# A fused attention and token-mixing block on one core: the last two blocks normalised by transposes into one tile, a ninth buffer for exponentials, and one planner policy for every stretch

## Chip, core and metric

The kernel runs on one core of one Trainium2 chip. The metric is the device time of one execution in microseconds (us), as the median of several runs. One execution was also taken by the hardware profiler. Its span is the time from the program's first to its last profiled instruction.

## What is computed

One token sequence of S = 2048 rows and D = 512 columns is normalised twice and goes through multi-head attention (32 heads of 16 columns) and through a token-mixing MLP of width F = 1376. The results are added to the input:

```python
def _A_ref(x, wqkv, wo):
    B, S, D = x.shape
    H = 32; Dh = D // H
    qkv = (lambda x, *d: x.transpose(*d))((x @ wqkv).reshape(B, S, 3, H, Dh), 2, 0, 3, 1, 4)
    q, k, v = qkv[0], qkv[1], qkv[2]
    scores = jnp.einsum("bhqd,bhkd->bhqk", q, k) * Dh ** -0.5
    p = _softmax(scores, axis=-1)
    o = jnp.einsum("bhqk,bhkd->bhqd", p, v)
    return (lambda x, *d: x.transpose(*d))(o, 0, 2, 1, 3).reshape(B, S, D) @ wo

def _B_ref(x, w1, b1, w2, b2):
    h = _layernorm(x, axis=-1)
    u = _gelu(jnp.einsum("bsd,sf->bdf", h, w1) + b1)
    y = jnp.einsum("bdf,fs->bds", u, w2) + b2
    return (lambda x, *d: x.transpose(*d))(y, 0, 2, 1)

xn = _layernorm(A_x, axis=-1)
return A_x + _A_ref(xn, A_wqkv, A_wo) + _B_ref(xn, B_w1, B_b1, B_w2, B_b2)
```

Inputs, weights and the output are bfloat16.

## The kernel before

**Blocks and groups.** Queries are cut into 4 quarters of 512 rows (qb), heads into 8 sets of four (G). That makes 32 blocks (NBLK), numbered b = 8 qb + G. T = G // 2 is a tile of 128 columns of the heads' output, and e_ = G % 2 says which half of each 32 rows of that tile the block fills. A block has 16 groups (NKT), one for each 128 keys, 512 groups in all. A group's scores are four matmuls (score_mm, L678), one for each head, and each fills one PSUM bank of 512 columns.

**Two paths for the exponentials.** A group goes one of two ways. On ScalarE it takes two ACTIVATE instructions (exp_tile, L701), each over two banks, into one of NPB = 8 buffers of pT; two more buffers lie in xn_sb once that tile is free (NPX = 2), which the profile shows as `xn_sb<-ps` on L701. The other path approximates the exponential with integer arithmetic on the bits of bfloat16 numbers: VectorE copies each of the four banks with a scale and a bias into a "plane" (dve_first, L761, or two banks at once in dve_first2, L769), and two further planes are made by adding a constant, by VectorE (add_plane, L774) or GpSimd (add_plane_pool, L781). Planes lie in tiles that have become free (x_sb, xn_sb, plx, h_sb, w1blk, wqkv_sb, xnT). TensorE then multiplies each buffer, or each of the three planes, by V (pv_mm, L714), four 32-column matmuls at a time, and adds up in PSUM bank 6 (PV_BANK). V17 has a column of ones for each head, so row 16 of each 32 rows of the sum is the softmax denominator. V17b is the same, scaled for the third plane.

**The order.** The order of all instructions is worked out on the host when the program is built: a dispatcher steps a clock for each engine, with an estimated occupancy and latency for each operation, and appends an instruction to its engine's stream when its inputs should be there. On the chip each engine runs its stream in order and waits on semaphores. pe_step decides what TensorE does next: scores for ScalarE if one of ScalarE's two PSUM slots should be free, scores for the other path if a bank of 4, 5 and 7 is, or else a "unit" of four 32-column matmuls (a PV product, a step of a projection, of the MLP or of the output projection; pe_fill). A tuple of 16 numbers (TOL, JOIN, DEFER and so on) sets tolerances and preferences. POLICY holds such a tuple for every 10 us of planned time (SEG), 65 in all. Which groups go which way falls out of this: ScalarE takes the next group whenever it can, d_pick1 chooses for the other path.

**Between the blocks.** chain_epi normalises a block: VectorE copies PV_BANK into OT32 (cp, L1286); SP gathers the four denominator rows through DRAM into den_s, 16 numbers on each of 128 partitions (gather, gather2; LAT_I is the planner's latency for the latter); VectorE takes the reciprocal (L1301); SP writes it back and broadcasts it into denb (out1, and bcast with four DMAs); GpSimd multiplies OT32 by denb (L1323), for e_ = 0 into oT, for e_ = 1 into otmp, from where four DMAs (join, o_join) put it beside the other half in oT. Queries are brought to rows of QT by eight DMAs (q_rows).

**The end.** For the last four row tiles (12 to 15, here c = 0 to 3), chain_yo adds the MLP's result, the first PT[c] of four pieces of the output projection and the input into part. The remaining pieces (op_mm, T = PT[c] to 2) are added in bank TBANK[c]. For c in HL the value of part is split into a high and a low bfloat16 half on GpSimd (part_split) and added by two matmuls with the identity (part_mm), so that ScalarE can copy the bank out; for the others VectorE adds part on the way out (L2028). The last piece, T = 3, comes from blocks 30 and 31 in two products with zero-padded halves of the weights (op_half with wo_pad): e_ = 0 reads block 30's result in oT, e_ = 1 reads block 31's in otmp. Block 31 has no DMA chain: tail_epilogue transposes PV_BANK in 32 x 32 pieces (L1994), so that the denominators stand beside their numbers, takes reciprocals (L1999), multiplies into gT (L2003) and transposes back into otmp (L2008). The rows of the output go out by SP, the last by ScalarE's queue.

The gelu of the MLP runs once, in the middle, as two ACTIVATEs (L1062) between two loads of ScalarE's function tables.

## Time and profile before

| | |
|---|---|
| median of 3 runs | 657.51 us (657.49 to 657.55) |
| the profiled execution's own time | 657.41 us |
| its span | 655.6 us, TensorE's granted clock 0.999 |
| ScalarE (ACT) busy | 643.6 us, 98% |
| TensorE (PE) busy | 643.7 us, 98% |
| VectorE (DVE) busy | 616.6 us, 94% |
| GpSimd (POOL) busy | 424.2 us, 65% |

Busy times are unions: instructions of one engine that overlap are counted once. Matmuls are pipelined, so TensorE's share is no measure of its load. PEld are its weight loads. A row of the costliest groups gives the line, the engine, the operation, what it writes and reads with shapes, the count, the busy time and the mean of one instruction in ns, and, behind the second bar, the idle time just ahead of them with what ended it. A row of the timeline gives the start, the duration in us, the line and how many equal instructions were merged.

### The profile page before, as it was taken

To read this page: it belongs to the slowest core of one execution; us is meant where nothing else is said; L and a number is where in the kernel's file an instruction comes from. 1 tells how busy PE (TensorE), PEld (TensorE's weight loads), DVE (VectorE), ACT (ScalarE), POOL (GpSimd) and SP (SyncE) were. 2 spreads that over 40 slices of the span, in tenths; PEclk is the share of its full clock that TensorE was granted. 3 is DMA by queue.
4 is the path that set the end of the run, shared out by engine and by line. 5 is a ranking of instruction groups with operands and counts; after the bars stand their busy time and mean duration, and the time that the engine had idled before them with its cause. 6 is when DMAs were issued, how large, how long until landed. Compare 5 with 4: busy or idle time off the path is not lost.

```text
span 655.6 us, 20689 instructions
## 1 busy us (share of the span) xinstructions
PE 643.7 (98%) x8873; PEld 189.8 (29%) x8873; DVE 616.6 (94%) x1071; ACT 643.6 (98%) x702; POOL 424.2 (65%) x292
## 2 busy tenths in 40 slices
PE   8999999999999999999999999999999999999997
PEld 4533333322222222222222222222222222222222
DVE  7989999989999999999999999999999999999997
ACT  7999999999999999999999999999999999999996
POOL 5631567575675657554856877977787566676772
PEclk9999999999999999999999999999999999999999
DMA  7015110122222212220122222112011131312101
GB/s 225 4 52 110 28 41 4 31 51 54 56 44 58 51 28 55 51 40 19 29 57 54 56 57 57 43 45 70 22 50 26 32 78 34 90 43 59 36 24 51
DMA packets 77002, 32.99 MB, mean 50 GB/s; under 512 B 61618, under 2 KB 72818, under 8 KB 76910
## 3 DMA queue, kind: packets, MB, share of 16 engines
q1 hardware_dynamic: 76478, 31.27, 19.0%
q8 instruction: 70, 1.15, 0.7%
q10 hardware_dynamic: 432, 0.39, 0.2%
q14 instruction: 22, 0.18, 0.1%
HBM read 26.08 MB, written 2.61 MB: 44 GB/s over the span
## 4 chain that ended last, share of the span: by engine, by line
ACT 76%; PE 19%; DVE 2%; DMA 1%; POOL 0%; issue 0%; DVEq 0%; POOLq 0%
ACT pT L701 74%; PE ps L678 7%; PE ps L714 7%; PE ps L611 5%; ACT gT L1062 1%; ACT xn_sb L701 1%; DMA den_s<-den_scr 0%; DVE stats L528 0%; DMA x_sb<-in_A_x_dram 0%; POOL mv L549 0%; DVE xn_sb L566 0%; DMA den_scr<-OT 0%; DVE x_sb L761 0%; ACT L701 0%; ACT L1062 0%
## 5 line engine op out<-in xcount | busy, mean ns | idle before, releaser
L701 ACT ACTIVATE pT<-ps 128x1024 bf16<-128x1024 f32 x682 | 626.9, 1136 | 1.1 <-PE ps L678 0.9
L678 PE MATMUL ps<-QT,KT 32*128 32x512 bf16 x2048 | 277.4, 384 | 6.7 <-ACT pT L701 5.0
L678 PEld LDWEIGHTS ps<-QT,KT 32*128 32x128 bf16 x2048 | 71.4, 90 | 280.3 <-ACT pT L701 267.5
L714 PE MATMUL ps<-pT,V 128*32 128x512 bf16 x1364 | 132.4, 388 | 0.1
L761 DVE TENSOR_SCALAR x_sb<-ps 128x512 int16<-128x512 f32 x190 | 125.0, 684 | 7.8 <-PE ps L678 6.2
L761 DVE TENSOR_SCALAR xn_sb<-ps 128x512 int16<-128x512 f32 x140 | 92.6, 685 | 6.6 <-PE ps L678 5.3
L761 DVE TENSOR_SCALAR plx<-ps 128x512 int16<-128x512 f32 x104 | 68.5, 684 | 4.5 <-PE ps L678 3.8
L611 PE MATMUL ps<-h_sb,w1blk 128*32 128x512 bf16 x688 | 57.7, 383 | 0.0
L611 PE MATMUL ps<-gT,w2blk 128*32 128x512 bf16 (+1 forms) x704 | 56.2, 383 | 0.1
L714 PEld LDWEIGHTS ps<-pT,V 128*32 128x32 bf16 x1364 | 33.8, 94 | 62.6 <-issue 59.4
L761 DVE TENSOR_SCALAR xnT<-ps 128x512 int16<-128x512 f32 x72 | 47.4, 685 | 2.2 <-PE ps L678 1.5
L761 DVE TENSOR_SCALAR wqkv_sb<-ps 128x512 int16<-128x512 f32 x68 | 44.7, 684 | 2.1 <-PE ps L678 1.6
L611 PE MATMUL ps<-xnT,wqkv_sb 128*32 128x512 bf16 (+2 forms) x568 | 40.4, 355 | 0.1
L761 DVE TENSOR_SCALAR w1blk<-ps 128x512 int16<-128x512 f32 x56 | 36.1, 684 | 2.4 <-PE ps L678 2.1
L714 PE MATMUL ps<-x_sb,V 128*32 128x512 bf16 x380 | 36.1, 383 | 0.0
L781 POOL TENSOR_TENSOR x_sb<-x_sb,shift_w 128x1024 int32<-128x1024 int32 x14 | 26.5, 1891 | 14.3 <-DVE x_sb L761 6.3
L781 POOL TENSOR_TENSOR x_sb<-xn_sb,shift_w 128x1024 int32<-128x1024 int32 x9 | 17.0, 1892 | 25.7 <-PE ps L678 18.3
L781 POOL TENSOR_TENSOR xn_sb<-x_sb,shift_w 128x1024 int32<-128x1024 int32 x13 | 24.5, 1893 | 7.6 <-DVE plx L774 2.8
L714 PE MATMUL ps<-xn_sb,V 128*32 128x512 bf16 x292 | 28.7, 383 | 0.0
L1323 POOL TENSOR_TENSOR oT<-OT,denb 128x512 bf16<-128x512 f32 x16 | 20.4, 1275 | 12.5 <-DVE w1blk L774 7.0
L781 POOL TENSOR_TENSOR x_sb<-plx,shift_w 128x1024 int32<-128x1024 int32 x11 | 20.8, 1891 | 10.7 <-DVE plx L761 3.6
L761 DVE TENSOR_SCALAR h_sb<-ps 128x512 int16<-128x512 f32 x40 | 26.2, 685 | 1.4 <-PE ps L678 1.2
(197 smaller groups left out, 883.2 us busy)
## 6 DMA issues: line engine op xcount, KB each, us to landing
denb<-rec_scr SPq DMA_DIRECT2D x124, 64.0 KB, 2.0
w1blk<-in_B_w_dram SPq DMA_DIRECT2D x10, 512.0 KB, 5.4
w2blk<-in_B_w_dram SPq DMA_DIRECT2D x16, 320.0 KB, 3.3
xres<-in_A_x_dram SPq DMA_DIRECT2D x16, 128.0 KB, 2.2
QT<-qst SPq DMA_DIRECT2D x120, 16.0 KB, 1.8
out_dram<-osb SPq DMA_DIRECT2D x14, 128.0 KB, 1.7
wqkv_sb<-in_A_wqkv_dram SPq DMA_DIRECT2D x3, 384.0 KB, 7.8
x_sb<-in_A_x_dram SPq DMA_DIRECT2D x2, 512.0 KB, 6.8
```

Source lines behind the costliest of these rows:

```text
L611: return e.matmul(dst[a:b, :], lhsT=lhsT[:, a:b], rhs=rhs, start=start, stop=stop, **pos)
L678: return sc.add("pe", lambda e: e.matmul(bank(bk), lhsT=KT[32 * r:32 * r + 32, T, 128 * kt:128 * (kt + 1)], rhs=QT[32 * r:32 * r + 32, slo ...
L701: return sc.add("act", lambda e: e.activation(pT_buf(buf), ps[:, slot * 1024:(slot + 1) * 1024], ACTF.Exp, scale=EXP_SCALE), reads=[("bank ...
L714: return sc.add("pe", lambda e: e.matmul(bank(PV_BANK)[32 * r:32 * r + 32, :], lhsT=vt_[:, off:off + 32], rhs=rhs, start=start, stop=stop, ...
L761: return sc.add("dve", lambda e: e.tensor_scalar(plane_i[pb][:, 512 * r:512 * (r + 1)], bank(bk), BIAS, 0.0, ALU.add, ALU.max), reads=[("b ...
L781: return sc.add("pool", lambda e: e.tensor_tensor(plane_w[pb], plane_w[pb0], shift_w[:, j:j + 1].broadcast_to([128, 1024]), ALU.add), read ...
L1062: op = sc.add("act", lambda e, m=m, f0=f0, f1=f1: e.activation(gT[0:m, f0:f1, :], gT[0:m, f0:f1, :], ACTF.Gelu_apprx_tanh), reads=[("gT", ...
L1323: op = sc.add("pool", lambda e: e.tensor_tensor(dst, OT32[:, eb, :], denb[:, :], ALU.mult), reads=[("OT32", eb)] + [("denb", r) for r in r ...
```

## The change

- NPB is 9 instead of 8: one more buffer of pT.
- POLICY holds one tuple, used for all of planned time, in place of 65.
- The planner's estimates: a DMA occupies its queue for 632 ns in q_rows and o_join and for 560 ns in den_g (name of gather), where it was 450 for all; LAT_I is 3800 ns instead of 4300.
- Block 30 is normalised by chain_turn instead of chain_epi: VectorE transposes PV_BANK into denb, takes the reciprocal and multiplies into columns 0 to 15 of each 32 of otmp's second half. Block 31's result goes into columns 16 to 31 of the same tile, and two transposes bring both blocks together into oT. The last piece of the output projection is then one product with wo_c (op_last) for each of the four row tiles; wo_pad, its memset and its eight loads go.
- HL is (0, 2) and PT is (1, 2, 1, 2): row tiles 0 and 2 go out by ScalarE, 1 and 3 by VectorE, and a split waits for its own part alone (part_of).
- In tail_epilogue the remaining output matmuls are all put ahead of the last products.

```diff
@@ -57,7 +57,7 @@
 BITS_MAX = float(0x7F80)
 
 DEBUG_SCHED = False
-NPB = 8
+NPB = 9
 NPX = 2
 NQS = 4
 NW1 = 2
@@ -94,73 +94,7 @@
 
 
 SEG = 10000.0
-POLICY = [
...
-]
+POLICY = [(120.0, 200.0, 400.0, -1, 0, 1300.0, 0.0, 0.05, 2, 3, 2, 7500.0, 0, 0.0, 1000.0, 2)]
 
 
 SWITCH = 95.0
@@ -376,7 +310,6 @@
         wqkv_sb = wqkv_flat[:, :].rearrange("p (j c n) -> p j c n", j=3, c=NCT)
         qmask = sb("qmask", [128, 2], F32)
         wo_c = sb("wo_c", [128, 4, D], BF16)
-        wo_pad = sb("wo_pad", [128, 2, D], BF16)
         KT = sb("KT", [128, 4, S], BF16)
         QT = sb("QT", [128, NQS, 512], BF16)
         V17 = sb("V17", [128, NKT * H * 17 + 16], BF16)
@@ -433,7 +366,8 @@
             else:
                 def fn(eng, dst=dst, src=src):
                     return eng.dma_start(dst, src)
-            op = sc.add(q, fn, reads=reads, writes=writes, name=name, dma=True, out_dma=out_dma, occ=450.0, lat=lat)
+            op = sc.add(q, fn, reads=reads, writes=writes, name=name, dma=True, out_dma=out_dma,
+                        occ={"q_rows": 632.0, "o_join": 632.0, "den_g": 560.0}.get(name, 450.0), lat=lat)
 
             dma_free[0] = max(dma_free[0], op.start + 1300.0) + move
             op.end = max(op.end, dma_free[0] + 700.0)
@@ -442,7 +376,7 @@
 
         NPRE = 4
         TABLE = 1490.0
-        LAT_I, LAT_B = 4300.0, 3100.0
+        LAT_I, LAT_B = 3800.0, 3100.0
 
 
         sc.add("pool", lambda e: e.memset(ident[:], 0.0), writes=[("ident",)], occ=200, lat=430)
@@ -506,16 +440,9 @@
         MLAST = F - 128 * NFTF
 
         def late_consts():
-            sc.add("pool", lambda e: e.memset(wo_pad[:], 0.0),
-                   writes=[("wo_pad", e_, r) for e_ in range(2) for r in range(4)], occ=900)
             sc.add("dve", lambda e: e.memset(gT[96:97, NFT - 1, :], 1.0), writes=[("gT1",)], occ=500)
             dma("sp", wo_c[:, :, :], A_wo.rearrange("(T q) n -> q T n", q=128), reads=[], writes=[("wo_c",)],
                 name="ld_wo")
-            for e_ in range(2):
-                for r in range(4):
-                    row = 3 * 128 + 32 * r + 16 * e_
-                    dma("sp", wo_pad[32 * r:32 * r + 16, e_, :], A_wo[row:row + 16, :], reads=[],
-                        writes=[("wo_pad", e_, r)], name="ld_wop")
             sc.add("pool", lambda e: e.memset(b1r[:], 0.0), writes=[("b1r",), ("b1r2",)], occ=120, lat=230)
             dma("sp", b1r[0:NFT - 1, :], B_b1[0:128 * (NFT - 1)].rearrange("(ft p) -> ft p", p=128),
                 reads=[], writes=[("b1r",)], name="ld_b1a")
@@ -907,6 +834,7 @@
         ge_done = [1e18]
         yo_done = {qb: 0 for qb in range(NQB)}
         part_done = [0]
+        part_of = set()
         oT_done = {qb: set() for qb in range(NQB)}
         mul_done = [0]
         bc_done = [0]
@@ -1080,19 +1008,17 @@
             return mm(bank(bk), oT[:, par, T, 128 * sti:128 * (sti + 1)], wo_c[:, T, :], first, last,
                       [("oT", par, T), ("wo_c",)] + [("oTj", par, T, r) for r in range(4)], [("bank", bk)])
 
-        def op_half(par, e_, sti, bk, first, last):
-            src = oT[:, par, 3, 128 * sti:128 * (sti + 1)] if e_ == 0 else otmp[:, par_o(NBLK - 1), 128 * sti:128 * (sti + 1)]
-            key = ("oT", par, 3) if e_ == 0 else ("otmp", par_o(NBLK - 1), sti)
-            return mm(bank(bk), src, wo_pad[:, e_, :], first, last, [key] + [("wo_pad", e_, r) for r in range(4)],
+        def op_last(sti, bk):
+            return mm(bank(bk), oT[:, 1, 3, 128 * sti:128 * (sti + 1)], wo_c[:, 3, :], False, True, [("oTL", sti), ("wo_c",)],
                       [("bank", bk)])
 
         def par_o(b):
             return (b // 2) % 2
 
 
-        HL = (0, 1)
-
-        PT = (1, 1, 2, 2)
+        HL = (0, 2)
+
+        PT = (1, 2, 1, 2)
         TBANK = (4, 5, EX_BANK, 0)
         hl_done = [0]
         hilo = xnT_flat[:, 2048 * (NQB - 1):].rearrange("p (t n) -> p t n", n=512)
@@ -1174,6 +1100,7 @@
                                 writes=[("part", sti)] + [("h", t) for t in range(4 * sti // 2, 4 * sti // 2 + 2)],
                                 **T_DVE(512))
                     part_done[0] += 1
+                    part_of.add(sti)
                     return op
 
                 def gate():
@@ -1342,6 +1269,32 @@
             if e_ == 1:
                 steps.append(Step("sp", join))
             return Chain("epi%d" % b, steps, -1.0, 0.0)
+
+
+
+        def chain_turn(b):
+            dn = denb[:, :].rearrange("p (c m) -> p c m", m=32)
+            wt = otmp[:, 1, :].rearrange("p (c m) -> p c m", m=32)
+            dk = [("denb", r) for r in range(4)]
+
+            def cp():
+                op = sc.add("dve", lambda e: e.transpose(denb[:, :], bank(PV_BANK)), reads=[("bank", PV_BANK)], writes=dk,
+                            **T_DVE(512))
+                pv_block[0] = b + 1
+                pv_open[0] = True
+                return op
+
+            def rec():
+                return sc.add("dve", lambda e: e.reciprocal(den_s[:, 0, :], dn[:, :, 16]), reads=dk, writes=[("den_s", 0)],
+                              occ=100, lat=230)
+
+            def mul():
+                mul_done[0] += 1
+                return sc.add("dve", lambda e: e.tensor_tensor(
+                    wt[:, :, 0:16], dn[:, :, 0:16], den_s[:, 0, :].rearrange("p (c o) -> p c o", o=1).broadcast_to([128, 16, 16]),
+                    ALU.mult), reads=dk + [("den_s", 0)], writes=[("otmp", 1, c) for c in range(4)], two=True, **T_DVE(256))
+            return Chain("epi%d" % b, [Step("dve", cp, 610, gate=lambda: mul_done[0] >= b), Step("dve", rec, 100),
+                                       Step("dve", mul, 340, two=True)], -1.0, 0.0)
 
 
         ex_queue.append(chain_k1(-2.0))
@@ -1375,7 +1328,7 @@
             yo_pos[12 + i] = (28.05 + 0.75 * i, 0.75)
         for idx, st in enumerate(yt_order):
             ex_queue.append(chain_yo(st, yo_pos[st][0] + yo_pos[st][1], yo_pos[st][0], idx))
-        bg.append(Chain("hilo", [Step("pool", lambda c=c, j=j: part_split(c, j), gate=lambda c=c: part_done[0] >= (2 if c < 2 else 4)
+        bg.append(Chain("hilo", [Step("pool", lambda c=c, j=j: part_split(c, j), gate=lambda c=c: c in part_of
                                       and (NQB - 1, 3) in qt_done) for c in HL for j in range(2)], NBLK - 1.0, 0.0))
         bg.append(Chain("gelu", [Step("act", gelus, gate=lambda: ut_done[0] == NFT)], 0.0, 0.0))
         bg.append(chain_ln2r(1.0))
@@ -1427,8 +1380,6 @@
                     z.append((bk, lambda c=c, bk=bk, j=j: part_mm(c, j, bk),
                               lambda c=c, j=j: hl_done[0] > HL.index(c)
                               and sc.ready(reads=[("hilo", HL.index(c), j)]) <= now[0]))
-            z.append((bk, lambda c=c, bk=bk: op_half(1, 0, c, bk, False, False),
-                      lambda: len(oT_done[3]) == NG - 1 and sc.ready(reads=[("oT", 1, 3)]) <= now[0]))
             tail["steps"].append(z)
 
         def d_over():
@@ -1659,7 +1610,7 @@
             if last:
                 pv_open[0] = False
                 if b < NBLK - 1:
-                    bg.append(chain_epi(b))
+                    bg.append(chain_turn(b) if b == NBLK - 2 else chain_epi(b))
                     bg[-1].t = sc.streams["pe"][-1].end
                     bg[-1].due = -1.0
 
@@ -1977,47 +1928,40 @@
 
 
         def tail_epilogue():
-            b = NBLK - 1
-            po = par_o(b)
 
             NB = 256 // 32
             dt = pT[:, 0, :].bitcast(F32)
             dn = dt.rearrange("p (c m) -> p c m", m=32)
-            wt = gT[:, 0, :].rearrange("p (c m) -> p c m", m=32)
+            wt = otmp[:, 1, :].rearrange("p (c m) -> p c m", m=32)
 
             def half(hf):
                 cols, blks = slice(256 * hf, 256 * hf + 256), slice(NB * hf, NB * hf + NB)
-                return (cols, blks, den_s[:, 0, blks], ("denT", hf), ("denS", hf), ("gTt", hf))
+                return (cols, blks, den_s[:, 1, blks], ("denT", hf), ("denS", hf), ("wt", hf))
 
             for hf in range(2):
                 cols, blks, rc, dk, sk, wk = half(hf)
                 sc.add("dve", lambda e, cols=cols: e.transpose(dt[:, cols], bank(PV_BANK)[:, cols]),
-                       reads=[("bank", PV_BANK)], writes=[dk] + ([("pT", 0)] if hf == 0 else []),
-                       **T_DVE(256))
+                       reads=[("bank", PV_BANK)], writes=[dk] + ([("pT", 0)] if hf == 0 else []), **T_DVE(256))
             for hf in range(2):
                 cols, blks, rc, dk, sk, wk = half(hf)
                 sc.add("dve", lambda e, rc=rc, blks=blks: e.reciprocal(rc, dn[:, blks, 16]), reads=[dk],
-                       writes=[sk] + ([("den_s", 0)] if hf == 0 else []), occ=100, lat=230)
+                       writes=[sk] + ([("den_s", 1)] if hf == 0 else []), occ=100, lat=230)
             for hf in range(2):
                 cols, blks, rc, dk, sk, wk = half(hf)
                 sc.add("dve", lambda e, rc=rc, blks=blks: e.tensor_tensor(
-                    wt[:, blks, 0:16], dn[:, blks, 0:16], rc.rearrange("p (c o) -> p c o", o=1).broadcast_to([128, NB, 16]),
-                    ALU.mult), reads=[dk, sk], writes=[wk] + ([("gT", 0)] if hf == 0 else []), **T_DVE(128))
+                    wt[:, blks, 16:32], dn[:, blks, 0:16], rc.rearrange("p (c o) -> p c o", o=1).broadcast_to([128, NB, 16]),
+                    ALU.mult), reads=[dk, sk], writes=[wk], **T_DVE(128))
             for hf in range(2):
                 cols, blks, rc, dk, sk, wk = half(hf)
-                sc.add("dve", lambda e, cols=cols: e.transpose(otmp[:, po, cols], gT[:, 0, cols]), reads=[wk],
-                       writes=[("otmp", po, c) for c in (2 * hf, 2 * hf + 1)], **T_DVE(256))
-
+                sc.add("dve", lambda e, cols=cols: e.transpose(oT[:, 1, 3, cols], otmp[:, 1, cols]),
+                       reads=[wk] + [("otmp", 1, c) for c in (2 * hf, 2 * hf + 1)],
+                       writes=[("oTL", c) for c in (2 * hf, 2 * hf + 1)]
+                       + ([("oT", 1, 3)] + [("oTj", 1, 3, r) for r in range(4)] if hf == 0 else []), **T_DVE(256))
             for z in tail["steps"]:
-                while len(z) > 1:
+                while z:
                     z.pop(0)[1]()
-            for hf in range(2):
-                tr = sc.streams["dve"][hf - 2].end
-                for z in list(tail["steps"]):
-                    while z and (z[0][0] in TBANK[2 * hf:2 * hf + 2] or sc.free["pe"] + 226.0 <= tr):
-                        z.pop(0)[1]()
-                for c in (2 * hf, 2 * hf + 1):
-                    op_half(1, 1, c, TBANK[c], False, True)
+            for c in range(4):
+                op_last(c, TBANK[c])
             for c in range(4):
                 st = 12 + c
                 bk = TBANK[c]
```

65 rows, old and new, of the table POLICY are left out of this document.

## The prediction, made before the changed kernel was run

> **What bounds the kernel now.** I read the page first: busy time, the chain that ended last and the costliest group.
>
> ```profile
> span 655.6 us, 20689 instructions
> ...
> PE 643.7 (98%) x8873; PEld 189.8 (29%) x8873; DVE 616.6 (94%) x1071; ACT 643.6 (98%) x702; POOL 424.2 (65%) x292
> ...
> ACT 76%; PE 19%; DVE 2%; DMA 1%; POOL 0%; issue 0%; DVEq 0%; POOLq 0%
> ...
> L701 ACT ACTIVATE pT<-ps 128x1024 bf16<-128x1024 f32 x682 | 626.9, 1136 | 1.1 <-PE ps L678 0.9
> ```
>
> Three engines look full, but the chain is ScalarE's exponentials (L701): these 682 and four into a spare tile, 686 in all. They overlap, so the mean of one (1136 ns) is not its price. ScalarE's own timeline and waits say how tightly they stand:
>
> ```profile
> 9.99 50.98 ACT L701 ACTIVATE pT<-ps 128x1024 bf16<-128x1024 f32 x55 [0.21 <-PE ps L678]
> ...
> 629.71 18.57 ACT L701 ACTIVATE pT<-ps 128x1024 bf16<-128x1024 f32 x20
> 651.20 1.08 ACT L595 ACTIVATE osb<-ps 128x512 bf16<-128x512 f32 x2 [2.93 <-PE ps L611]
> ```
>
> ```profile
> ACT pT L701 <- PE ps L678: 0.9, 2, 0.7
> ```
>
> From 9.99 to 648.27 us ScalarE runs exponentials without a break that counts: one stretch for gelu (8.74 us from start to start, with two table loads) and 0.9 us of waiting. From the starts of the single instructions in the trace: 411 of 685 distances round to 900 ns, and their median is 904 ns, the floor; without gelu and the one distance of 1.79 us the mean is 917.4 ns. So lateness over the floor is 683 x 13.4 ns = 9.2 us, and 0.9 us at the long distance. Time is thus 686 x 0.904 us, plus that lateness, plus a head of 10 us, gelu, and 7.3 us behind the last exponential. The profiled run took 657.41 us, 1.81 us over its span; the median shown is 657.51, 0.10 more.
>
> **The change part by part.** The planner splits 512 groups of scores between ScalarE (two exponentials each) and a path of VectorE and GpSimd (four copies and two further planes each). The order of the two programs' instructions on each engine settles what one policy for all stretches does to that split: 343 groups on ScalarE and 169 on the other path before, 348 and 164 after.
>
> Exponentials: 696 for 686, ten more on the engine that never rests: 10 x 0.904 = **+9.04 us**. The Trainium skill ("ScalarE: Activation LUTs", section "What ACT_TABLE_LOAD costs") gives an ACTIVATE with immediates 186 ns + 0.833 ns an element, and 93 ns of overlap back to back; as an estimate that is 946 ns here, 9.46 us for ten. The trace's floor is 904 ns, so its row decides.
>
> What is taken off the other path: VectorE has 656 single copies of scores for 670 (684 ns each), none of three double ones (1.22 us), and 159 plane additions for 147 (0.69 us): 8.3 - 9.6 - 3.7 = -5 us. GpSimd has 169 planes for 191, -22 x 1.89 = -42 us. Neither is on the chain; GpSimd was idle 35% of the span. This relief is worth nothing while ScalarE is late with nothing else.
>
> Lateness: it arises on TensorE, between two pairs of scores for ScalarE. Timeline near the end:
>
> ```profile
> 646.61 0.39 PE L678 MATMUL ps<-QT,KT 32*128 32x512 bf16 x2
> ...
> 646.92 0.40 PE L714 MATMUL ps<-pT,V 128*32 128x512 bf16 x4
> ...
> 647.15 0.39 PE L714 MATMUL ps<-h_sb,V17b 128*32 128x512 bf16 x4
> ...
> 647.37 0.39 PE L714 MATMUL ps<-plx,V 128*32 128x512 bf16 x4
> ```
>
> A pair takes 0.31 us from start to start, a unit of four matmuls 0.22. Pair and two units are 0.75 us, under the floor; with three it is 0.97, over it. Sorting before's distances by the units ahead of each pair bears this out: 124 with three units are late by 47.6 ns on average (5.90 us), 511 with fewer by 4.5 ns (2.29 us), 47 with small projections by 20.8 ns (0.98 us): the 9.2 us again. In the changed order there are 120, 517 and 54 of these, and three with four units, which I price at 0.31 + 4 x 0.22 - 0.904 = 0.29 us each: 5.71 + 2.33 + 1.12 + 0.87 = 10.03, so **+0.86 us**. Bounds: -1 (three-unit gaps land on time more often) and +2 (four-unit gaps meet late copies as well).
>
> The ninth buffer lets exponentials run further ahead of the matmuls that read them. ScalarE waited only twice, 0.9 us together, and the longer of these has another cause:
>
> ```profile
> 294.81 0.25 DVE L1301 RECIPROCAL den_s<-den_s 128x16 f32<-128x16 f32 x1 [0.85 <-DMA den_s<-den_scr]
> ...
> 295.67 0.38 PE L678 MATMUL ps<-QT,KT 32*128 32x512 bf16 x1 [0.35 <-DVE plx L761]
> ...
> 297.24 1.94 ACT L701 ACTIVATE pT<-ps 128x1024 bf16<-128x1024 f32 x2 [0.65 <-PE ps L678]
> ```
>
> A reciprocal stood in VectorE's queue before its denominators had landed; the copies behind it came late, a score waited for their bank, and ScalarE's next pair stood behind that score. 0.85 us on VectorE became 0.89 us on ScalarE. So the buffer is worth nothing; I take zero, between 0 and -0.25.
>
> LAT_I lets the planner place reciprocals 0.5 us earlier; the longer occupancies of q_rows, o_join and den_g place them later where the queue is crowded. In before three more of the 31 reciprocals had under 0.5 us between landing and start (0.13, 0.32, 0.46). If all move by 0.5: 0.37 + 0.18 + 0.04 + 0.5 = 1.1 us worse; if the longer occupancies cure all, 0.9 better. I take zero, one such stall as before.
>
> Block 30's tail: seven DMAs, a copy (0.68), a reciprocal (0.24) and a GpSimd multiply (1.28) give way to a transpose of 512 columns (two of 256 took 0.43 each: 0.68 to 0.86), a reciprocal (0.24) and a multiply of 256 (0.27 to 0.54). Some 0.4 us more on VectorE, hidden since the last block has six groups on that path instead of seven (four copies and a few planes less, over 3 us). The transpose overwrites denb, so it waits for block 29's multiply on GpSimd; behind it on VectorE stand score copies, and behind those TensorE's banks. In before that multiply ran from 632.6 to 633.9 while block 30's copy began at 633.1: a wait of 0.8 us there if nothing moved. In the new order 18 copies, five planes and three smaller instructions, some 16.7 us, stand between block 29's copy and the transpose, against 15.5 us from copy to end of multiply in before. I take zero; bounds 0 and +0.8.
>
> wo_pad's memset (0.95 us at 41.2) and eight loads (issued from 43.6 to 46.9 us) go: zero, since behind them on SP stand w1's load at 48.1, first read by TensorE at 125.6 us, and block 0's denominators, whose reciprocal started 8.6 us after they landed.
>
> Behind the last exponential:
>
> ```profile
> 648.27 0.40 PE L714 MATMUL ps<-w1blk,V17b 128*32 128x512 bf16 x4
> ...
> 648.50 0.39 PE L714 MATMUL ps<-pT,V 128*32 128x512 bf16 x4
> ...
> 648.94 0.78 DVE L1994 STREAM_TRANSPOSE pT<-ps 128x256 f32<-128x256 f32 x2 [0.73 <-PE ps L714]
> ...
> 650.75 0.62 PE L611 MATMUL ps<-wo_pad,otmp 128*32 128x512 bf16 x8
> ...
> 652.06 1.29 DVE L2028 TENSOR_TENSOR xres<-ps,h_sb 128x512 bf16<-128x512 f32 x2 [1.04 <-PE ps L611]
> ...
> 653.38 0.35 ACTq L435 DMA_DIRECT2D out_dram<-xres  x1
> ```
>
> The last pT unit stood behind a plane's unit; now it is the only one left, and starts about 0.05 instead of 0.23 us behind its exponential: -0.2. After the final transposes four units of op_last replace eight, and HL = (0, 2) gives VectorE rows 1 and 3: the first add can start at 650.75 + 0.22 + 0.40 + 0.04 = 651.41 instead of 652.06, two adds of 0.645 end 0.65 earlier, and the last store with them. Together **-0.8 us**; bounds -0.85 and +0.5 (ScalarE's last pair now stands behind a unit that waits for VectorE's last plane).
>
> Sum: 9.04 + 0.86 - 0.8 = +9.1, so 657.41 + 9.1 = **666.5 us**.
>
> **The rivals.** *VectorE's waits multiply*: the reciprocals' 1.1, the transpose's 0.8 and another two stalls like that of 295 us (1.8) make +3.7, 670.2 us. For it: any lateness on VectorE came through to ScalarE one to one. Against: 30 of 31 reciprocals did not wait, and VectorE has 5 us less to do. 13%.
>
> *Not slower*: better packing of TensorE by one order and one more buffer takes the lateness away. All of it is 10.1 us; with the ten exponentials and the tail the result is 657.41 + 9.04 - 0.8 = 665.65 less what is saved, so it decides from 8.2 us saved; all saved gives 655.6. Against: 5.9 us are three-unit gaps, and the order still has 120 of them. 3%.
>
> *The clock falls*: TensorE has 56 matmuls fewer over a longer time. At half clock pair and two units take 1.5 us instead of 0.75, and ScalarE is 0.6 us late for each of some four exponentials in 3.4 us: +2.4 us a lapse, 669 with one. The clock row is full throughout (mean 0.999), and both orders hold equally many zero matmuls. The Trainium skill ("TensorE: Matmul & The Clock Gate", section "Part 1: The HAM clock gate") says that an idle window of about 3.4 us halves the clock; the trace shows no such lapse here. 3%.
>
> *It does not do what it says*: no gain behind the last exponential at all; 667.3, inside my range and the forecast's chance.
>
> **How the numbers follow.** Forecast 81%: 666.5, own range by the bounds 664.5 to 669. With most of the first rival the range is **664.5 to 670.5**. A change of 0.2% (1.3 us) is about what measuring this kernel can tell: faster 0.02, same 0.01 (both the rival that is not slower), slower 0.97.
>
> **What would show it.** Right: 696 exponentials, from 9.99 to about 658.2 us, mean distance about 918 ns, one or two waits of ScalarE, under 7 us behind the last. GpSimd near 60% and VectorE under 94% busy without use. Wrong: a mean distance near 905 ns; a transpose or a reciprocal of VectorE waiting over 1 us with a gap of ScalarE behind it; a clock row under 9.

## The result, and the profile after

The changed kernel takes **667.38 us** (median of 4 runs, 667.34 to 667.74) against 657.53 for the kernel before beside it (657.49 to 657.74): a ratio of 1.015, with a 95% interval of 1.0133 to 1.0168. The forecast was 666.5, in a range of 664.5 to 670.5. The profiled execution took 667.39 us, 1.8 over its span.

The page of the changed kernel: span, busy time of each engine, the chain that ended last, and the costliest group. Its line numbers differ from those of before: exponentials L701 are now L628, scores L678 are L605, PV products L714 are L641, the VectorE copies of scores L761 are L688, and the projections' matmuls L611 are L538.

```profile
span 665.6 us, 20535 instructions
...
PE 645.9 (97%) x8817; PEld 190.7 (29%) x8817; DVE 613.4 (92%) x1067; ACT 653.4 (98%) x712; POOL 381.2 (57%) x268
...
ACT 79%; PE 16%; DVE 3%; POOL 1%; issue 1%; DMA 0%; DVEq 0%; POOLq 0%
...
L628 ACT ACTIVATE pT<-ps 128x1024 bf16<-128x1024 f32 x689 | 634.1, 1130 | 1.5 <-PE ps L605 1.4
```

ScalarE's exponentials are 689 here and seven into the spare tile, 696 in all. VectorE and GpSimd are busy for less time than before, and the span is 10 us longer: their relief bought nothing that shows. ScalarE's own timeline (an entry runs until a wait that counts) and its line in the waits:

```profile
10.08 5.68 ACT L628 ACTIVATE pT<-ps 128x1024 bf16<-128x1024 f32 x6 [0.21 <-PE ps L605]
16.16 38.88 ACT L628 ACTIVATE pT<-ps 128x1024 bf16<-128x1024 f32 x42 [0.39 <-PE ps L605]
...
126.00 186.31 ACT L628 ACTIVATE pT<-ps 128x1024 bf16<-128x1024 f32 x203 [0.64 <-PE ps L605]
...
628.91 29.59 ACT L628 ACTIVATE pT<-ps 128x1024 bf16<-128x1024 f32 x32
```

```profile
ACT pT L628 <- PE ps L605: 1.4, 4, 0.6
```

The last exponential ends at 628.91 + 29.59 = 658.50 us, against 648.27 before, 10.23 later. From the starts of the single exponentials:

| part of the 10.23 us | measured | forecast |
|---|---|---|
| start of the first (10.08 for 9.99) | +0.09 | 0 |
| ten more x 0.904 | +9.04 | +9.04 |
| lateness over the 904 ns floor (9.87 for 9.17) | +0.70 | +0.86 |
| single long distances, over the floor (1.42 and 1.69 for 1.79) | +0.42 | 0 |
| the distance with gelu | +0.05 | 0 |
| duration of the last one (1.08 for 1.15) | -0.07 | 0 |

Behind the last exponential the span has 7.09 us left, 0.25 less than before's 7.34, where 0.8 less was forecast.

### The profile page after: what moved, and what is told of

It is laid out like the page before. It is cut to its first block, busy times and chain, and to the rows that moved or that the text cites. A ratio compares the mean times of both kernels' runs of the same rounds, so it can differ in the third digit from the quotient of the medians.

```text
span 665.6 us, 20535 instructions
## 1 busy us (share of the span) xinstructions
PE 645.9 (97%) x8817; PEld 190.7 (29%) x8817; DVE 613.4 (92%) x1067; ACT 653.4 (98%) x712; POOL 381.2 (57%) x268
## 3 DMA queue, kind: packets, MB, share of 16 engines
q8 instruction: 69, 1.13, 0.7%
## 4 chain that ended last, share of the span: by engine, by line
ACT 79%; PE 16%; DVE 3%; POOL 1%; issue 1%; DMA 0%; DVEq 0%; POOLq 0%
ACT pT L628 77%; PE ps L605 6%; PE ps L641 5%; PE ps L538 5%; ACT xn_sb L628 1%; ACT gT L990 1%; DVE stats L455 1%; PE ps L537 1%; DMA x_sb<-in_A_x_dram 0%; DVE V L524 0%; DVE plx L688 0%; POOL h_sb L708 0%; POOL mv L476 0%; DVE xn_sb L493 0%; DVE xnT L524 0%
## 5 line engine op out<-in xcount | busy, mean ns | idle before, releaser
L628 ACT ACTIVATE pT<-ps 128x1024 bf16<-128x1024 f32 x689 | 634.1, 1130 | 1.5 <-PE ps L605 1.4
L605 PE MATMUL ps<-QT,KT 32*128 32x512 bf16 x2048 | 281.0, 384 | 9.5 <-ACT pT L628 7.8
L605 PEld LDWEIGHTS ps<-QT,KT 32*128 32x128 bf16 x2048 | 73.1, 91 | 284.9 <-ACT pT L628 270.6
L641 PE MATMUL ps<-pT,V 128*32 128x512 bf16 x1378 | 131.9, 388 | 2.4 <-DVE V L524 1.3
L688 DVE TENSOR_SCALAR x_sb<-ps 128x512 int16<-128x512 f32 x164 | 107.0, 681 | 7.6 <-PE ps L605 6.7
L688 DVE TENSOR_SCALAR xn_sb<-ps 128x512 int16<-128x512 f32 x132 | 85.8, 682 | 7.0 <-PE ps L605 6.4
L688 DVE TENSOR_SCALAR plx<-ps 128x512 int16<-128x512 f32 x96 | 63.1, 682 | 3.8 <-PE ps L605 3.0
L688 DVE TENSOR_SCALAR xnT<-ps 128x512 int16<-128x512 f32 x80 | 51.9, 680 | 5.7 <-PE ps L605 5.3
L538 PE MATMUL ps<-h_sb,w1blk 128*32 128x512 bf16 x688 | 55.2, 384 | 0.0
L538 PE MATMUL ps<-gT,w2blk 128*32 128x512 bf16 (+1 forms) x704 | 55.1, 384 | 0.0
L688 DVE TENSOR_SCALAR h_sb<-ps 128x512 int16<-128x512 f32 x76 | 49.3, 678 | 4.3 <-PE ps L605 3.9
L688 DVE TENSOR_SCALAR wqkv_sb<-ps 128x512 int16<-128x512 f32 x76 | 49.5, 683 | 3.9 <-PE ps L605 3.4
L641 PEld LDWEIGHTS ps<-pT,V 128*32 128x32 bf16 x1378 | 33.3, 94 | 62.6 <-issue 55.4
L538 PE MATMUL ps<-xnT,wqkv_sb 128*32 128x512 bf16 (+2 forms) x568 | 40.0, 355 | 0.6 <-DVE xnT L524 0.3
L641 PE MATMUL ps<-x_sb,V 128*32 128x512 bf16 x352 | 33.7, 383 | 0.0
L708 POOL TENSOR_TENSOR plx<-x_sb,shift_w 128x1024 int32<-128x1024 int32 x10 | 18.9, 1892 | 20.2 <-DVE wqkv_sb L701 9.7
L641 PE MATMUL ps<-xn_sb,V 128*32 128x512 bf16 x290 | 29.4, 382 | 0.2 <-DVE V L524 0.2
L708 POOL TENSOR_TENSOR x_sb<-x_sb,shift_w 128x1024 int32<-128x1024 int32 x10 | 18.9, 1891 | 10.5 <-DVE x_sb L701 3.3
L1250 POOL TENSOR_TENSOR otmp<-OT,denb 128x512 bf16<-128x512 f32 x15 | 19.1, 1273 | 7.2 <-DVE plx L701 3.0
```

The costliest lines, as they stand in the source:

```text
L538: return e.matmul(dst[a:b, :], lhsT=lhsT[:, a:b], rhs=rhs, start=start, stop=stop, **pos)
L605: return sc.add("pe", lambda e: e.matmul(bank(bk), lhsT=KT[32 * r:32 * r + 32, T, 128 * kt:128 * (kt + 1)], rhs=QT[32 * r:32 * r + 32, slo ...
L628: return sc.add("act", lambda e: e.activation(pT_buf(buf), ps[:, slot * 1024:(slot + 1) * 1024], ACTF.Exp, scale=EXP_SCALE), reads=[("bank ...
L641: return sc.add("pe", lambda e: e.matmul(bank(PV_BANK)[32 * r:32 * r + 32, :], lhsT=vt_[:, off:off + 32], rhs=rhs, start=start, stop=stop, ...
L688: return sc.add("dve", lambda e: e.tensor_scalar(plane_i[pb][:, 512 * r:512 * (r + 1)], bank(bk), BIAS, 0.0, ALU.add, ALU.max), reads=[("b ...
L708: return sc.add("pool", lambda e: e.tensor_tensor(plane_w[pb], plane_w[pb0], shift_w[:, j:j + 1].broadcast_to([128, 1024]), ALU.add), read ...
```

## The experiments

Each ratio is to runs of the kernel before on the same chip, taken beside it.

### Which part moves the split: one_policy, eight_buffers, tail_alone, old_policies

one_policy is the kernel before with the changed kernel's single tuple:

```
-POLICY = [
-    (130.0, 150.0, 300.0, -1, 0, 1300.0, 0.0, 0.05, 2, 3, 2, 7500.0, 0, 0.0, 1000.0, 2),
...
-]
+POLICY = [(120.0, 200.0, 400.0, -1, 0, 1300.0, 0.0, 0.05, 2, 3, 2, 7500.0, 0, 0.0, 1000.0, 2)]
```

> The kernel before with the single policy alone; buffers, estimates and the end as before. Its order has 696 exponentials on ScalarE, ten more than before. Theory A (the time follows the number of exponentials, and the split is lost because the 65 policies had been fitted to one particular program): 657.5 + 10 x 0.904 = 666.6, give or take 1.5 us of lateness. Theory B (the new end, the transposes and the ninth buffer cost the time, the policy little): 657.5 to 660.

Measured: 668.19 us (667.98 to 668.4), ratio 1.016 [1.014, 1.0181], 696 exponentials; 0.1 us above the range of theory A, and far from theory B. The single policy alone gives the changed kernel's number of exponentials and, to within 0.8 us, its time. The changed estimates for DMAs, which had no run of their own, are not in it.

eight_buffers is the changed kernel without the ninth buffer:

```
-NPB = 9
+NPB = 8
```

> The changed kernel with eight buffers instead of nine. Its order has 696 exponentials, as the changed kernel. If the ninth buffer does nothing: 667.4 give or take 1 us. If it hides lateness of TensorE: 669 or more.

Measured: 668.06 us (667.4 to 668.72), ratio 1.0153 [1.0106, 1.02], again 696 exponentials. Its interval holds the changed kernel's 1.015: no effect of the buffer can be told. Its slower execution is the profiled one; the granted clock was 0.50 there for 3.4 us from 524.8, and two distances there were 1.4 us over the floor together. The other execution took 667.4, the changed kernel's time.

tail_alone is the kernel before, with its 65 policies, and the new end:

```
-        wo_pad = sb("wo_pad", [128, 2, D], BF16)
...
-        def op_half(par, e_, sti, bk, first, last):
...
+        def op_last(sti, bk):
...
-        HL = (0, 1)
+        HL = (0, 2)
...
-        PT = (1, 1, 2, 2)
+        PT = (1, 2, 1, 2)
...
-                    bg.append(chain_epi(b))
+                    bg.append(chain_turn(b) if b == NBLK - 2 else chain_epi(b))
```

> The kernel before with the new end alone (transposes for block 30, one tile, op_last, HL and PT, no wo_pad); the 65 policies, eight buffers and the estimates as before. Its order has 698 exponentials. Theory A: two more than the changed kernel, 669.2 give or take 1.5 us, and more if loads come late as in old_policies; behind the last exponential 7.1 us. Theory B' (only the single policy costs): 657.

Measured: 670.44 us (669.74 to 671.13), ratio 1.0189 [1.0141, 1.0237], 698 exponentials. In the profiled execution the last exponential ended at 660.67 and 8.66 us followed, 1.3 more than in before, because the last stores took longer to land, and one of them to issue. The issue of the last two, on SP and on ScalarE's queue, and their landing (columns: KB each, us from issue to landing):

```profile
664.93 2.11 SPq L434 DMA_DIRECT2D out_dram<-xres  x1
664.96 0.36 ACTq L434 DMA_DIRECT2D out_dram<-xres  x1
```

```profile
out_dram<-xres SPq DMA_DIRECT2D x1, 128.0 KB, 3.8
out_dram<-xres ACTq DMA_DIRECT2D x1, 128.0 KB, 3.5
```

old_policies is the changed kernel with before's list of 65 tuples in place of the single one (the first diff turned round).

> The changed kernel with the 65 policies of before put back; everything else as changed. Its order has 700 exponentials. Theory A: four more than the changed kernel, 667.4 + 4 x 0.904 = 671.0, give or take 1.5 us. Theory B' (the single policy as such is the loss, so the old list gives it back): 657 to 659.

Measured: 674.71 us (673.26 to 676.16), ratio 1.0259 [1.0229, 1.029], 700 exponentials: the slowest of all, above theory A's 671.0 give or take 1.5, and far from theory B'. So the list is not good in itself. It gives 686 exponentials on the program of before and on one that differs from it only in the last stretch (end_on_old_order, below); with a slightly different program under it, the same list gives 698 or 700, more than the single policy does. Over and above its 14 exponentials this kernel lost 4.5 us, and the trace shows some of it. Timeline, then a table of windows (busy time of PE, PEld, DVE, ACT and POOL, granted clock, DMA share, GB/s):

```profile
619.96 0.62 PE L604 MATMUL ps<-gT,w2blk 128*32 128x512 bf16 x4 [2.37 <-DMA w2blk<-in_B_w_dram]
...
621.16 1.94 ACT L694 ACTIVATE pT<-ps 128x1024 bf16<-128x1024 f32 x2 [2.43 <-PE ps L671]
```

```profile
615.00:620.00 5.00, 2.63 (x37) 0.78 (x32) 4.30 (x7) 3.73 (x5) 3.03 (x3) 0.98 0.48 109
620.00:625.00 5.00, 5.00 (x52) 1.23 (x52) 1.24 (x3) 3.43 (x4) 0.41 (x1) 0.68 0.24 51
625.00:630.00 5.00, 5.00 (x66) 1.37 (x66) 3.53 (x6) 5.00 (x6) 0.73 (x1) 1.00 0.02 7
```

TensorE waited 2.37 us for a block of w2, ScalarE waited 2.43 us for the scores behind it, and the granted clock fell: it was 0.50 for 3.41 us from 619.77 on, just before that wait ended, which the second row shows as a mean of 0.68. The same execution has two more such falls, at 469.6 and 653.9 us.

### Is it the number of exponentials: refitted_split

The changed kernel with a list of 72 tuples, searched for its own program by the planner's planned end:

```
-POLICY = [(120.0, 200.0, 400.0, -1, 0, 1300.0, 0.0, 0.05, 2, 3, 2, 7500.0, 0, 0.0, 1000.0, 2)]
+POLICY = [
+    (120.0, 200.0, 400.0, -1, 0, 1300.0, 0.0, 0.05, 2, 3, 2, 7500.0, 0, 0.0, 1000.0, 2),
+    (120.0, 80.0, 400.0, -1, 0, 1300.0, 0.0, 0.05, 2, 3, 2, 7500.0, 0, 0.0, 1000.0, 1),
...
+]
```

> The changed kernel with a list of 72 policies, one for each stretch, searched for its own program by the planner's planned end, in place of the single one: 692 ScalarE exponentials and 166 VectorE groups instead of 696 and 164. Theory E (the time follows the number of exponentials that the plan gives ScalarE, 0.904 us each): four fewer are 3.6 us, so 663.8, give or take 1.5 us for lateness. Rival G (the number is only a sign; what costs is how the changed program runs): 666 us or more.

Measured: 663.67 us (662.41 to 664.16, 5 runs), ratio 1.0087 [1.0074, 1.0101], against 663.8 expected. The page of the profiled execution (662.41 us):

```profile
span 660.6 us, 20530 instructions
...
PE 645.2 (98%) x8813; PEld 191.4 (29%) x8813; DVE 615.3 (93%) x1068; ACT 649.4 (98%) x708; POOL 399.9 (61%) x278
...
L701 ACT ACTIVATE pT<-ps 128x1024 bf16<-128x1024 f32 x689 | 633.2, 1126 | 0.6 <-PE ps L678 0.6
```

With three into the spare tile that is 692. The last one ends at 653.53, 4.97 before the changed kernel's: 4 x 0.904 = 3.62 from the number, 0.78 because the long distance at 124 us is gone, 0.42 less lateness, the rest head and gelu. Rival G is refuted. GpSimd's busy time rises again with the two groups given back, as does VectorE's.

### Is the new end itself worth anything: end_on_old_order, end_old_order_stores, stores_swapped

end_on_old_order has the new end on the order of before: the edits of tail_alone, but wo_pad with its memset and loads stays, though nothing reads it, so that the order up to the last stretch is that of before. Its end, as in the changed kernel:

```
-            for hf in range(2):
...
-                    op_half(1, 1, c, TBANK[c], False, True)
+            for c in range(4):
+                op_last(c, TBANK[c])
```

> The kernel before with the changed end alone (block 30 by chain_turn, one output product per row tile, the single transpose back), and with what the order is planned from kept as it was: the 65 policies, the old estimates, eight buffers, and wo_pad with its loads, which nothing reads any more. So the order is that of before up to the last stretch: 686 ScalarE exponentials and 169 VectorE groups instead of 696 and 164. Theory E (the whole of the loss is the split of the exponentials; the end itself only gains): the last exponential ends at 648.3 us as in before, the rest takes 7.1 us as in the changed kernel instead of 7.34, so 657.0 to 657.5. Rival F (the new end's waits on denb and on the single tile cost time whatever the order): 658 us or more, with an exponential late behind them in the last 60 us.

Measured: 657.97 us (657.39 to 659.5, 11 runs), ratio 1.0001 [0.9989, 1.0014]. The page of the profiled execution (span and busy times), and the one wait of VectorE on denb:

```profile
span 656.2 us, 20645 instructions
...
PE 643.2 (98%) x8857; PEld 189.0 (29%) x8857; DVE 616.2 (94%) x1072; ACT 643.9 (98%) x702; POOL 425.0 (65%) x292
```

```profile
DVE denb L1354 <- POOL otmp L1323: 0.3, 1, 0.3
```

Busy times are those of before to within 1 us. The transpose of block 30 does wait for GpSimd, 0.3 us, but in the last 90 us of the profiled execution ScalarE has no wait before its first copy-out at 651.93. Rival F, 658 us or more with a late exponential there, is refuted in its mechanism; theory E's 657.0 to 657.5 was missed by half a microsecond. The part behind the last exponential is 7.07 us, as expected; the exponentials ended at 649.10 instead of 648.3, for which these windows show a cause that is not in the end of the program:

```profile
515.00:517.50 2.50, 1.98 (x22) 0.49 (x18) 2.36 (x4) 2.42 (x3) 2.50 (x2) 0.72 0.01 3
517.50:520.00 2.50, 2.50 (x26) 0.44 (x23) 1.19 (x2) 1.55 (x2) 2.02 (x2) 0.60 0.05 13
```

The granted clock fell to 0.72 and 0.60 on average, and two exponentials came 0.86 and 0.61 us late there; before's own long distance of 1.79 was 1.28 here.

This kernel and tail_alone differ in one thing: wo_pad with its memset and its eight loads, between 41 and 47 us, which nothing reads. With them in place the list of 65 tuples gives 686 exponentials and 657.97 us; without them 698 and 670.44. In the traces the order of TensorE's matmuls is that of before up to 591 us here, and up to 45 us in tail_alone. So what cost 12 us under the old list is not the new end but the order that the planner found once those loads were gone.

stores_swapped changes in the changed kernel which queue stores which of the last rows:

```
-                dma("act" if c == 3 else "sp", out2[128 * st:128 * (st + 1), :], buf[:, c % 2, :], reads=[key],
+                dma("act" if c == 2 else "sp", out2[128 * st:128 * (st + 1), :], buf[:, c % 2, :], reads=[key],
```

> The changed kernel with the queues of the last two stores exchanged: row tile 2 goes out by ScalarE's queue right after its copy, row tile 3 by SP. In the changed kernel both were issued within 0.03 us (662.82 and 662.85) and landed 2.2 and 1.9 us later, where before's last one took 1.7. If the two stores slow each other, the last now lands 0.3 to 0.5 us earlier: 666.9 to 667.1. If the landing has another cause: 667.4.

Measured: 667.2 us (667.14 to 667.23, 4 runs), ratio 1.0145 [1.0128, 1.0162]; in the profiled executions 6.93 us behind the last exponential instead of 7.09. The gain of 0.16 is below what was expected and what the ratios can tell.

end_old_order_stores has this edit on end_on_old_order.

> The kernel end_on_old_order with the stores of the last two row tiles exchanged between the queues of SP and ScalarE, as in stores_swapped. Theory E with the 0.16 us that the exchange was worth there: 656.9 to 657.3, under the kernel before by 0.2 to 0.6. Rival F: 658 us or more.

Measured: 657.39 us (656.8 to 661.66, 12 runs) beside 657.79 for the kernel before, ratio 1.0003 [0.9986, 1.0021]. The profiled execution's span is 655.29, 0.32 under the span shown of before, with the last exponential at 648.36 and 6.93 behind it. The median is 0.09 us above the range expected; it is 0.40 under the kernel before's, but the interval does not separate the two: no version was shown to beat that one.

### Does taking work out of ScalarE's order give the time back: short_ten, five_dropped, five_vector_dropped, both_dropped

short_ten cuts ten exponentials of the changed kernel to 64 of their 1024 columns and leaves the others out:

```
-            return sc.add("act", lambda e: e.activation(pT_buf(buf), ps[:, slot * 1024:(slot + 1) * 1024],
...
+            w = 64 if n_act_[0] % 60 == 59 and n_act_[0] < 600 else 1024
+            return sc.add("act", lambda e: e.activation(pT_buf(buf)[:, 0:w], ps[:, slot * 1024:slot * 1024 + w],
...
```

> The changed kernel, same order, with ten exponentials spread over the run cut to 64 of 1024 columns (the other columns' exponentials are left out). If ScalarE sets the time all along, each gives back between 0.45 us (the next but one pair of scores needs 0.45 us after the short one) and 0.75 us: 4.5 to 7.5 us in all, 660 to 663. If TensorE (97% busy) or VectorE is as near to being the bound, less than 2 us comes back: 665.4 or more.

Measured: 667.04 us (666.53 to 667.55), ratio 1.0143 [1.0122, 1.0163]. A short one takes 0.34 us, but from its start to the next start 0.78 to 1.03 us pass, 0.86 on average instead of 0.904: ten are worth under half a microsecond, and the profiled execution's last exponential ended no earlier (658.67; another distance of 1.68 us, at 17 us, took more than that). The theory that ScalarE alone sets the time had expected 4.5 to 7.5 us back and is refuted as it stood; the time lies where the other case had put it (less than 2 us back). One of the ten starts at 66.10, and the next full one is the last line:

```profile
65.56 0.45 PE L605 MATMUL ps<-QT,KT 32*128 32x512 bf16 x3
...
65.94 0.63 PE L538 MATMUL ps<-wqkv_sb,xnT 128*32 128x128 bf16 x32
...
66.50 0.39 PE L605 MATMUL ps<-QT,KT 32*128 32x512 bf16 x3
...
66.93 1.94 ACT L629 ACTIVATE pT<-ps 128x1024 bf16<-128x1024 f32 x2 [0.50 <-PE ps L605]
```

The next scores stand behind 32 matmuls in TensorE's order and start at 66.50, so ScalarE waits 0.50 us instead of computing. With two PSUM slots no later exponential was ready to take the place, and the saved time did not close up.

five_dropped takes five ScalarE groups out of the changed kernel's finished order (scores, exponentials and PV products; their keys are missing from five blocks), which leaves 686 exponentials:

```
+        CUT = (5, 10, 15, 20, 25)
...
+        sc.order = [o_ for o_ in sc.order if o_ not in cut_ops]
+        for e_ in sc.ENGS:
+            sc.streams[e_] = [o_ for o_ in sc.streams[e_] if o_ not in cut_ops]
```

> The changed kernel, same order, with five groups of scores of ScalarE's path taken out whole, one each in the blocks 5, 10, 15, 20 and 25: 20 score matmuls, ten exponentials and five units of PV are left out, so 686 exponentials remain as in before and VectorE's and GpSimd's work stays as in the changed kernel. Theory A (each pair of scores and its exponential is a turn of the loop that sets the time): 10 x 0.904 = 9.0 us come back, 657.5 to 659.5. Theory C (TensorE's sum is the bound; short_ten gave nothing back): only its share of these groups comes back, 5 x (2 x 0.31 + 0.22) = 4.2 us, 663.2.

Measured: 666.11 us (666.1 to 666.13), ratio 1.0123 [1.0083, 1.0164]: 1.3 us back, where ten exponentials are 9. Both theories' numbers were far off. The waits and one of the five places:

```profile
ACT pT L629 <- PE ps L605: 8.0, 9, 1.5
```

```profile
130.66 0.62 PE L538 MATMUL ps<-h_sb,w1blk 128*32 128x512 bf16 x8
...
131.21 0.38 PE L605 MATMUL ps<-QT,KT 32*128 32x512 bf16 x1
...
131.53 0.61 PE L538 MATMUL ps<-h_sb,w1blk 128*32 128x512 bf16 x8
...
132.07 0.39 PE L605 MATMUL ps<-QT,KT 32*128 32x512 bf16 x1
...
133.37 1.94 ACT L629 ACTIVATE pT<-ps 128x1024 bf16<-128x1024 f32 x2 [1.42 <-PE ps L605]
```

What was planned between the missing pairs still runs in its order: single scores for VectorE, each when VectorE has freed a bank, and units between them. ScalarE has two PSUM slots, so its next scores cannot be far ahead, and it waits 1.42 us here, 8.0 in all.

five_vector_dropped takes out five groups of the other path instead, by the same means (all 696 exponentials stay):

```
+        CUT, CUT_D = (), (85, 165, 246, 325, 405)
```

> The changed kernel, same order, with five groups of VectorE's path taken out whole (20 score matmuls, 20 copies, ten further planes and 15 units of PV; one group each in the blocks 5, 10, 15, 20 and 25). five_dropped gave back 1.3 us for five groups of ScalarE's path. Theory D (the two paths are each nearly full and the order ties them together, so relief of one alone is worth little): also little, 665.5 to 667.4. Theory E (VectorE's path is the one that sets the time, ScalarE only follows): 3 us or more each, 652 or less.

Measured: 669.62 us (667.95 and 671.29), ratio 1.018 [1.0119, 1.0242]; in the profiled execution (667.95) the last exponential ended at 659.06, 0.56 later than in the changed kernel. Theory E (652 or less) is refuted, and theory D's 665.5 to 667.4 was missed on the slow side: less work for VectorE and GpSimd alone gives no gain.

both_dropped takes out both kinds:

```
+        CUT, CUT_D = (5, 10, 15, 20, 25), (85, 165, 246, 325, 405)
```

> The same five groups of VectorE's path and the five groups of ScalarE's path of five_dropped, which stand next to them, taken out together. Theory D: together they give back what neither does alone, about 10 groups x 638 us / 512 = 12.5 us if the order could close up wholly, 6 to 12.5 us as it stands: 655 to 661. If the reliefs only add up: their sum, 664 to 666.

Measured: 663.65 us (663.01 and 664.3), ratio 1.009 [1.006, 1.0119]; the last exponential ended at 655.39, 3.11 earlier than in the changed kernel, while the single removals gave 1.27 and -0.56. Both expectations were missed: the time is just under the 664 to 666 for a mere sum, and well over the 655 to 661 for an order that closes up. Together the removals give more than their sum, which fits that five_dropped's places were held by both paths, but only a third of the 9 us came back. In this execution the granted clock was 0.50 from 337.05 to 340.47 us, and the two distances of 2.51 and 1.52 us around it took some of the gain; the other execution, which has no trace, took 1.29 us less.

The kernels whose order was planned anew, beside 657.5 + 0.904 x (number - 686):

| kernel | exponentials | by the floor alone | measured |
|---|---|---|---|
| end_on_old_order | 686 | 657.5 | 657.97 |
| refitted_split | 692 | 662.9 | 663.67 |
| changed kernel | 696 | 666.5 | 667.38 |
| eight_buffers | 696 | 666.5 | 668.06 |
| one_policy | 696 | 666.5 | 668.19 |
| tail_alone | 698 | 668.3 | 670.44 |
| old_policies | 700 | 670.2 | 674.71 |

## Why the prediction was right, and where it was off

**The ten exponentials.** Right. The term of 9.04 us carries the result, and every kernel planned with more exponentials is slower by at least the floor's price. What the removals add is a limit: 0.904 us is the price of an exponential in a plan, not what comes back when one is taken out of a finished order (0.05 us for a short one, 0.13 for a dropped one). So the term is a sound account of where the time went, but the number is not the lever by itself: the planner gives ScalarE the next group whenever it can, so a plan that is longer for any reason also has more exponentials. five_dropped has 686 of them, as before has, and takes 666.11 us. What in the single policy's order leaves five groups fewer to the other path is not shown. (By the trace 456 of before's 685 distances lie from 895 to 905 ns, where the forecast has 411 that round to 900; the median is 904, as it says.)

**The relief of VectorE and GpSimd.** Right that by itself it is worth nothing (five_vector_dropped); together with ScalarE's relief it gave 1.84 us more than that alone (both_dropped beside five_dropped). Where their time went shows in VectorE's waits, first of before, then of the changed kernel (us in total, times, longest):

```profile
DVE x_sb L761 <- PE ps L678: 6.2, 27, 0.4
DVE xn_sb L761 <- PE ps L678: 5.3, 20, 0.5
```

```profile
DVE x_sb L688 <- PE ps L605: 6.7, 19, 1.5
DVE xn_sb L688 <- PE ps L605: 6.4, 18, 1.0
DVE xnT L688 <- PE ps L605: 5.3, 13, 1.5
```

VectorE's idle time rose from 36.7 to 49.4 us over the span, and its pauses of over 0.5 us from 8 (7.6 us) to 20 (20.2 us): it waits longer for its scores. That these scores went to ScalarE in the plan is a reading, not shown. That the single policy gives this split is shown by one_policy; which of the 16 numbers does it was not tried.

**Lateness.** +0.70 for +0.86, but two of its parts were off and nearly cancel, which is luck. The 119 distances with three units were late by 48.0 ns (47.6 forecast). The three with four units, priced at 0.29 us each as TensorE's time over the floor, were late by 16 ns, 0.05 us in all instead of 0.87: that the lead of the two PSUM slots absorbs a single long gap fits this, but was not tested. The 516 with fewer cost 3.15 us, not 2.33, and the 53 with small projections 0.97, not 1.12.

**Reciprocals and the long distances.** Forecast: one stall as in before, at no change. No reciprocal held up a score in the changed kernel, and the two long distances have other causes, 0.42 us worse together. The larger:

```profile
124.04 0.40 PE L641 MATMUL ps<-pT,V 128*32 128x512 bf16 x4
...
124.49 0.69 DVE L524 CAST V<-ps 128x512 bf16<-128x512 f32 x1 [0.29 <-PE ps L641]
...
125.23 0.40 PE L641 MATMUL ps<-pT,V 128*32 128x512 bf16 x4 [0.80 <-DVE V L524]
125.57 0.65 PE L605 MATMUL ps<-QT,KT 32*128 32x512 bf16 x6
...
126.00 1.94 ACT L628 ACTIVATE pT<-ps 128x1024 bf16<-128x1024 f32 x2 [0.64 <-PE ps L605]
```

A copy of V came late on VectorE, a PV product waited 0.80 us for it, and ScalarE's scores stood behind that product: the mechanism of the rival with VectorE's waits, with a copy of V in the reciprocal's place. It came a second time: at 54.44 us a PV product waited 0.47 us for a copy of V, and ScalarE's distance there was 1.26 us, 0.36 over the floor (counted above with the lateness). TensorE's waits for such copies in the changed kernel (us in total, times, longest), where before shows none of this size:

```profile
PE ps L641 <- DVE V L524: 1.5, 3, 0.8
```

This step of the forecast named the wrong wait: one or two waits of ScalarE were forecast, and there are four, 1.4 us together.

**The ninth buffer, the transpose and wo_pad.** Zero for each of the first two was borne out as far as it can be told: eight_buffers differs from the changed kernel within its interval, and the transpose waited 0.3 us for block 29's multiply, inside the bounds of 0 and 0.8, with no wait of ScalarE behind it. For wo_pad the forecast looked at the waits behind its loads alone. Under before's list taking it out moved the whole order (tail_alone beside end_on_old_order, 12.5 us); under the single policy the number is 696 with it (one_policy) and without it.

**Behind the last exponential.** This is the mis-sized term: -0.25 us instead of -0.8, and 7.09 us where under 7 was forecast. The timeline up to the last stores and their landing:

```profile
658.62 0.39 PE L641 MATMUL ps<-pT,V 128*32 128x512 bf16 x4
...
659.06 0.78 DVE L1943 STREAM_TRANSPOSE pT<-ps 128x256 f32<-128x256 f32 x2 [2.77 <-PE ps L641]
...
660.86 1.05 PE L538 MATMUL ps<-wo_c,oT 128*32 128x512 bf16 x16 [1.21 <-DVE oT L1956]
...
661.53 0.69 DVE L1972 TENSOR_TENSOR osb<-ps,h_sb 128x512 bf16<-128x512 f32 x1 [0.40 <-PE ps L538]
...
662.82 0.45 SPq L368 DMA_DIRECT2D out_dram<-xres  x1
662.85 0.37 ACTq L368 DMA_DIRECT2D out_dram<-xres  x1
```

```profile
out_dram<-xres SPq DMA_DIRECT2D x1, 128.0 KB, 2.2
out_dram<-xres ACTq DMA_DIRECT2D x1, 128.0 KB, 1.9
```

On the engines the forecast held: the first add starts 3.03 us behind the last exponential instead of 3.79, and the last store is issued 4.35 us behind it instead of 5.11, 0.76 earlier. But two stores are now issued 0.03 us apart, and the later to land took 2.22 us; before's last took 1.73. The forecast ended its sum at the issue of the store and left the landing out; 0.5 us went there. With the two stores apart by 0.42 us (stores_swapped), both still took 2.1 us, so that these two were issued together is not shown to be the cause. A rival is that all of the last four stores share something: they were issued within 1.56 us in before and the last two took 1.79 and 1.73 to land, within 1.13 us in one_policy (1.86 and 1.98), and within 0.91 us here (2.22 and 1.94) and in stores_swapped (2.14 and 2.08). No run varies this alone. What the new end gains also depends on the order: the old end under the single policy (one_policy) has 7.11 us behind its last exponential, 0.02 more than the changed kernel.

**The rivals.** VectorE's waits did not multiply as that rival had it: no reciprocal waited, the transpose waited 0.3 us, and the two late copies of V cost 1.14 us. Nothing of the lateness was saved, so the case of not slower did not come. No fall of the clock shows in the changed kernel (mean 0.999, a full row); it fell in old_policies, eight_buffers, both_dropped and end_on_old_order, and in the last of these a lapse cost 1.47 us over the floor, not the 2.4 that the forecast worked out. The change does what it says, by 0.76 us on the engines.

## What to carry to other kernels

Where a planner fills one engine without a gap, count that engine's instructions in the two finished orders first: their difference times the distance of two starts carried nearly all of this result, whatever the diff was meant for. A list of tuned choices belongs to the one program that it was found on; edit the program, even by taking out eight loads that nothing reads, and the same list can be worse than one plain choice, so tune again or freeze the order (as end_on_old_order does) before judging the edit. And an instruction's price in a plan is not what its removal from a fixed order saves.

## What the runs showed of the hardware that was not expected

The granted clock can fall without a long pause of TensorE. Ahead of the fall to 0.72 and 0.60 in end_on_old_order, TensorE's pauses of over 0.12 us between 508 and 515.7 us were four, of 0.17, 0.20, 0.20 and 0.52 us; the profiled execution of the kernel before has four of 0.17, 0.20, 0.19 and 0.52 us at the same place, and its clock stayed at 1.00. The Trainium skill ("TensorE: Matmul & The Clock Gate", section "Part 1: The HAM clock gate") ties the fall, in its table of states, to an idle window of about 3.4 us; no such pause lies ahead of this one. The same part's account of a kernel whose clock swings because TensorE is often idle for a moment between groups of matmuls is nearer to it. The clock was 0.50 from 516.08 to 519.49 us, for 3.41 us, and each of the five falls in eight_buffers, both_dropped and old_policies was as long. In old_policies one of the three began 2.2 us into a pause of 2.37 us; ahead of the other two, and of those in eight_buffers and both_dropped, no pause of the 8 us before was over 0.53 us.

In refitted_split the runs with a mean clock of 0.997 took 663.67 to 664.16 us, one of 0.998 took 662.41 and one of 0.999 took 662.45: more than 1 us between executions of one program.

The last stores of these kernels, 128 KB each, took from 1.7 to 3.8 us to land, and their issue on SP from 0.36 to 2.11 us. The last store's landing is a term of the sum with a spread of its own.
